# Weight tiles issued ahead of the loads of v, conversions ungated and below attention, two groups ahead of the loop

## The chip, the cores and the metric

The kernel runs on one core of a Trainium2 chip (trn2). The time is that of one execution on the device in microseconds (us); it is compared as a median over several executions. TensorE (PE in the profile) multiplies matrices, VectorE (DVE) and ScalarE (ACT) work on elements, GpSimd (POOL) makes the constants, and SyncE (SP) issues every DMA, in one queue and in program order. Each engine executes its own instructions strictly in the order in which they were put down.

## What is computed

A block-sparse attention over 2 batches, 8 heads, 768 positions and a head size of 64, then two feed-forward layers over the 1536 tokens of 512 features:

```python
    k_sum = k.reshape(B, H, nb, block, D).max(axis=3)      # nb = 24 blocks of 32
    v_sum = v.reshape(B, H, nb, block, D).mean(axis=3)
    scores_l = scale * np.matmul(q, k.transpose(0, 1, 3, 2))
    mask_l = np.abs(pos[:, None] - pos[None, :]) < window  # window = 16
    scores_s = scale * np.einsum('bhsd,bhnd->bhsn', q, k_sum) + np.log(block)
    a = softmax(np.concatenate([np.where(mask_l, scores_l, -1e9), scores_s], axis=-1))
    x = np.matmul(a, np.concatenate([v, v_sum], axis=2))
    ...
    h = np.maximum(x @ w_in, 0.0)                          # d_ff = 2048
    x = h * h @ w_out
    ...
    xn = x / rms * rms_g
    g = xn @ w_gate                                        # d_ff = 1536
    out = g * sigmoid(g) * (xn @ w_val) @ w_out2
```

The weights come as 64-bit floats and are converted on the chip.

## The kernel before

**Attention** goes by groups of 128 tokens, twelve in all (g = 0 to 11), six for each batch. For a batch, `prep_k` transposes k into `kT` (tiles `kps`) and takes its block maxima, and `vmean` averages v over blocks with matmuls (tile `vmean`, copied to `vm`). For each pair of groups `qprep` transposes q (`qps`). For each group `scores` multiplies (tiles `s`), `softmax` works on DVE and ACT (tile `t`), `ptrans` transposes the result (`pps`, copied to `pT`), and `av` multiplies it with the values (`xps`) and splits the sum into `xhi` (ACT) and `xlo` (DVE). The values of a group lie in `vx`, four slots that two groups share: `vload` brings the 96 rows of each half group from v, `vmfix` copies the 24 rows of summaries from `vm` into each slot. The rows of the summaries stay in the slots, so `vmfix` is called for the first two groups of a batch alone.

**The weights** pass through a list (`units1`): first `wi` 0 to 3 and `wo` 0 to 3, then the others. A tile is loaded raw in 512 KB (`load64`, lines 160 and 164). `tick()` then does one step for up to three tiles: `conv_a` (two instructions on ACT, lines 175 and 176), `conv_b` (four on DVE, lines 182, 183, 186 and 189) and `split` (a cast on ACT, line 195, and a subtraction on DVE, line 196). So one tile costs three instructions on ACT and five on DVE.

**The first layer** is worked in rounds over its 16 tiles of `d_ff`; the first round holds four. In it a step takes two groups at a time: `h` (48 matmuls of 256 columns for a pair of groups, `product`, line 621), `r` (relu on ACT, line 769, and the square on DVE, line 770), `hsplit` (`hhi` on ACT, line 632, `hlo` on DVE, line 633), and `y` (24 matmuls of 512 columns, `ff_out`, line 642). `h_0_0` is the first half of `h` for the pair of groups 0 and 1, `h_0_2` its second half, `y_0_0` and `y_0_1` are the sums of these two groups. While this round runs, `Attention.point` puts one step of the attention of later groups between the products. The other two rounds and the second layer (`g`, `v`, `z`) follow.

**What sets the order.** The program is written in one sequence, and a scheduler orders each engine's instructions by priority. Every call of `Attention.point` raises the priority of what it emits by `LIFT` instructions. `after(...)` holds the instructions of a block back until a marked instruction has been issued: before, ten ticks are gated in that way behind the exponentials, the transposes and the splits of groups 0 and 1. Three groups (0, 1 and 2) are written out by hand ahead of the loop, and the loop starts at group 3.

Memory for raw tiles and for converted tiles comes from one ring of 14 (`wpool`, tag "w"); a tile that is to be loaded waits until the tile that had its place has been read.

Of the kernel before, what the change touches and what calls it, by code (L numbers as in the profile page):

```python
# [32 lines left out]
def tile_window_attention_moe_moe2(  # L33
# [210 lines left out]
    def NENG(g):  # L244
# [3 lines left out]
    QB = 2  # L248
    E0, E1 = 2, 3
    GN = (3, 1, 2, 1)  # L250
    GATES = sum(
        (
            [g] * n
            for g, n in zip(
                (
                    (("exp", 1), ("norm", 1)),
                    (("pT", 1), ("norm", 1)),
                    (("xhi", 0, 1), ("xlo", 0, 1)),
                    (("xhi", 1, 1), ("xlo", 1, 1)),
                ),  # L260
                GN,
            )
        ),
        [],
    )
    WARM, VM1 = 10, 1
    LIFT, POINTS = 120, 5
    WOLAG = 2
# [25 lines left out]
    NVX = 4  # L294
    vx = [ap_.tile([NK, H, D], F32, name=f"vx{i}") for i in range(NVX)]
    psX = actx.enter_context(tc.tile_pool(name="psX", bufs=2, space=PSUM))
# [113 lines left out]

    def vmfix(g):
        if g % GPB >= NVX // 2:
            return
        vm = state["vm"].rearrange("n (h d) -> n h d", h=H)
        for u in range(2):
            t = vx[(2 * g + u) % NVX]
            for j, a in ((WIN, u), (K0 + QT, 1 - u)):
                nc.sync.dma_start(t[j : j + GAP], vm[GAP * a : GAP * (a + 1)])

    def vload(g):  # L420
        b, r = divmod(g, GPB)
        for u in range(2):
            t = vx[(2 * g + u) % NVX]
            t0 = r * P + u * QT
            for j, n, o in ((0, WIN, t0 - WIN), (K0, QT, t0), (K1, WIN, t0 + QT)):
                o = min(max(o, 0), S - n)
                nc.sync.dma_start(t[j : j + n], v[b, :, o : o + n, :].rearrange("h s d -> s h d"))  # L427

# [73 lines left out]
    def av(g):  # L502
        pT = state.pop(("pT", g))
        ps = psA(f"xps1_{g}")
        for u in range(2):
            for p in range(NPAIR):
                o = p * P + QT * u
                for e in range(2):
                    nc.tensor.matmul(  # L509
                        ps[QT * e : QT * e + QT, o : o + QT],  # L510
                        vx[(2 * g + u) % NVX][:, 2 * p + e, :],
                        pT[:, e * NPAIR + p, QT * u : QT * u + QT],
                        start=True, stop=True,
                    )
# [9 lines left out]
    def pieces(g):  # L524
# [37 lines left out]
        def sc():  # L562
            scores(g)
            vload(g)
            softmax(g)
            vmfix(g)

# [11 lines left out]
    class Attention:  # L579
# [3 lines left out]
        def point(self, limit):  # L583
# [7 lines left out]
            for s_ in self.live:  # L591
# [3 lines left out]
                if need is None:  # L595
                    if s_.g >= limit:
                        continue
                elif not all(k_[0] in ("scores", "av") and k_[1] < 3 or k_ in state for k_ in need):
                    continue
# [12 lines left out]

    att = Attention(3)

# [86 lines left out]
    for c in range(NC2):  # L701
        prep_load(0, c)
    qload(0)
    for c in range(NC2):
        if c < E0:
            units1.load(c + 1)
        vm_load(0, c)
    for j in (0, LK - WIN):
        nc.gpsimd.memset(kT[:, :, j : j + WIN], 0.0)
# [5 lines left out]
    qprep(0)  # L715
    for c in range(VM1):
        vmean(0, c)
    prep_kend(0, 1)
    scores(0)
    with after(("s", 0)):  # L720
        for c in range(VM1, NC2):
            vmean(0, c)
    vload(0)
    vmfix(0)
    vload(1)
    vmfix(1)
    qload(2)
    softmax(0)
    with after(("s", 0)):
        scores(1)  # L730
    units1.ahead = 0
    for _ in range(E1):
        units1.tick()
    qprep(2)
    ptrans(0)
    softmax(1)
    scores(2)
    av(0)
    ptrans(1)
    vload(2)  # L740
    av(1)
    rot["tags"] = ("a", "x")
    softmax(2)
    ptrans(2)
    av(2)
    units1.ahead = 6
    for t in GATES:
        with after(*t):
            units1.tick()

# [175 lines left out]
```

## Time and profile before

| | |
|---|---|
| time, median of 3 runs | 704.88 us (701.39 to 708.34) |
| the profiled execution | 704.73 us, its span 703.0 us |
| instructions | 9371 |
| mean granted clock of TensorE | 0.969 |
| PE, DVE, ACT busy in the span | 668.5 us (95%), 408.4 us (58%), 307.2 us (44%) |

The span reaches from the first to the last instruction; 1.73 us of the execution lie around it. PE is busy for 95% of the span, which is an average over a beginning that is not bound by PE and a long rest that is, so the stretches are read one by one.

### The profile page before, as it was taken

To read this page: it belongs to the slowest core of one execution; us is meant where nothing else is said; L and a number is where in the kernel's file an instruction comes from. 1 tells how busy PE (TensorE), PEld (TensorE's weight loads), DVE (VectorE), ACT (ScalarE), POOL (GpSimd) and SP (SyncE) were. 2 spreads that over 40 slices of the span, in tenths; PEclk is the share of its full clock that TensorE was granted. 3 is DMA by queue.
4 is the path that set the end of the run, shared out by engine and by line. 5 is a ranking of instruction groups with operands and counts; after the bars stand their busy time and mean duration, and the time that the engine had idled before them with its cause. 6 is when DMAs were issued, how large, how long until landed. Compare 5 with 4: busy or idle time off the path is not lost.

```text
span 703.0 us, 9371 instructions
## 1 busy us (share of the span) xinstructions
PE 668.5 (95%) x3644; PEld 540.3 (77%) x3644; DVE 408.4 (58%) x735; ACT 307.2 (44%) x624; POOL 4.0 (1%) x25
## 2 busy tenths in 40 slices
PE   6687899888999999999999999999999999999997
PEld 5375676677888888888888888888888888888885
DVE  4798655555699938952838398349932152213122
ACT  4663254665576625622635486246721132111110
POOL 2000000000000000000000000000000000000000
PEclk9958799999999999999999999999999999999999
DMA  9589135222370321300114025014300000001011
GB/s 246 122 256 249 24 88 179 57 74 68 102 229 0 121 90 60 91 30 1 61 54 126 19 76 176 0 51 131 119 1 0 1 1 0 1 0 61 1 60 61
DMA packets 78236, 54.22 MB, mean 77 GB/s; under 512 B 46128, under 2 KB 72752, under 8 KB 78192
## 3 DMA queue, kind: packets, MB, share of 16 engines
q1 hardware_dynamic: 78192, 53.62, 25.9%
q8 instruction: 29, 0.48, 0.3%
q14 instruction: 15, 0.12, 0.1%
HBM read 50.07 MB, written 3.15 MB: 76 GB/s over the span
## 4 chain that ended last, share of the span: by engine, by line
PE 84%; ACT 4%; DVE 4%; SPq 4%; DMA 3%; issue 1%; DVEq 0%; ACTq 0%
PE y L642 18%; PE h L621 16%; PE g L621 14%; PE v L621 14%; PE z L642 14%; ACT t L468 3%; PE xps L509 2%; SPq L427 2%; DMA raw_wi<-in_moe_w_in_dram 2%; PE s L439 2%; SPq L327 1%; PE pps L488 1%; DVE t L462 1%; PE vmean L401 1%; PE xps L521 1%
## 5 line engine op out<-in xcount | busy, mean ns | idle before, releaser
L621 PE MATMUL h<-xhi,w_wi 128*128 128x512 f32 (+1 forms) x480 | 135.3, 356 | 0.8 <-ACT xhi L499 0.7
L642 PE MATMUL y<-w_wo,hhi 128*128 128x512 f32 x384 | 122.5, 404 | 7.7 <-ACT hhi L632 4.7
L872 DVE TENSOR_TENSOR sg<-v,sg 128x512 f32<-128x512 f32 x36 | 24.9, 692 | 132.8 <-PE v L621 132.8
L621 PEld LDWEIGHTS h<-xhi,w_wi 128*128 128x128 f32 x480 | 86.8, 195 | 13.9 <-ACT xhi L499 1.2
L621 PE MATMUL g<-xhi,w_wg 128*128 128x512 f32 x288 | 95.7, 393 | 0.0
L621 PE MATMUL v<-xhi,w_wv 128*128 128x512 f32 x288 | 95.7, 393 | 0.0
L642 PEld LDWEIGHTS y<-w_wo,hhi 128*128 128x128 f32 x384 | 73.0, 192 | 25.6 <-ACT hhi L632 5.1
L642 PE MATMUL z<-w_wp,hhiz 128*128 128x512 f32 x288 | 88.6, 392 | 0.0
L621 PE MATMUL h<-xlo,w_wi 128*128 128x512 f32 (+1 forms) x240 | 85.6, 357 | 1.6 <-DVE xlo L500 1.6
L642 PE MATMUL y<-w_wo,hlo 128*128 128x512 f32 x192 | 75.8, 402 | 1.6 <-DVE hlo L633 1.6
L870 ACT ACTIVATE sg<-g 128x512 f32<-128x512 f32 x36 | 21.5, 598 | 100.6 <-PE g L621 100.3
L621 PEld LDWEIGHTS g<-xhi,w_wg 128*128 128x128 f32 x288 | 54.1, 188 | 12.4
L621 PEld LDWEIGHTS v<-xhi,w_wv 128*128 128x128 f32 x288 | 54.1, 188 | 12.2
L642 PEld LDWEIGHTS z<-w_wp,hhiz 128*128 128x128 f32 x288 | 54.1, 188 | 11.9
L769 ACT ACTIVATE r<-h 128x512 f32<-128x512 f32 x48 | 28.5, 595 | 65.9 <-PE h L621 65.9
L621 PE MATMUL g<-xlo,w_wg 128*128 128x512 f32 x144 | 56.7, 394 | 0.0
L621 PE MATMUL v<-xlo,w_wv 128*128 128x512 f32 x144 | 56.6, 393 | 0.0
L642 PE MATMUL z<-w_wp,hloz 128*128 128x512 f32 x144 | 55.4, 393 | 0.0
L621 PEld LDWEIGHTS h<-xlo,w_wi 128*128 128x128 f32 x240 | 46.7, 194 | 8.1 <-DVE xlo L500 1.9
L632 ACT CAST hhiz<-sg 128x512 fp32r<-128x512 f32 x36 | 22.3, 620 | 66.4 <-DVE sg L872 66.0
L770 DVE TENSOR_TENSOR r<-h,r 128x512 f32<-128x512 f32 x48 | 32.9, 688 | 28.0 <-ACT r L769 27.9
L642 PEld LDWEIGHTS y<-w_wo,hlo 128*128 128x128 f32 x192 | 36.5, 192 | 10.1 <-DVE hlo L633 2.0
(125 smaller groups left out, 916.3 us busy)
## 6 DMA issues: line engine op xcount, KB each, us to landing
raw_wi<-in_moe_w_in_dram SPq DMA_DIRECT2D x16, 512.0 KB
raw_wo<-in_moe_w_out_dram SPq DMA_DIRECT2D x16, 512.0 KB
raw_wg<-in_moe_w_gate_dram SPq DMA_DIRECT2D x12, 512.0 KB
raw_wv<-in_moe_w_val_dram SPq DMA_DIRECT2D x12, 512.0 KB
raw_wp<-in_moe_w_out_dram SPq DMA_DIRECT2D x12, 512.0 KB
kr<-in_k_dram SPq DMA_DIRECT2D x12, 256.0 KB
qr<-in_q_dram SPq DMA_DIRECT2D x12, 256.0 KB
vr<-in_v_dram SPq DMA_DIRECT2D x6, 512.0 KB
```

Source lines behind the costliest of these rows:

```text
L327: nc.sync.dma_start(t[:, j].rearrange("p (h d) -> p h d", h=H), src[b, :, o : o + P, :].rearrange("h p d -> p h d"),)
L427: nc.sync.dma_start(t[j : j + n], v[b, :, o : o + n, :].rearrange("h s d -> s h d"))
L439: mark[("s", g)] = nc.tensor.matmul(sl[e][QT * u : QT * u + QT, p, :], qT[rr, p, QT * u : QT * u + QT], kT[rr, p, o : o + NK], start=True, ...
L468: mark[("exp", g)] = nc.scalar.activation(t[:, h], t[:, h], AF.Exp, bias=mx[:, h : h + 1], accum_out=sm[:, h : h + 1])
L509: nc.tensor.matmul(ps[QT * e : QT * e + QT, o : o + QT], vx[(2 * g + u) % NVX][:, 2 * p + e, :], pT[:, e * NPAIR + p, QT * u : QT * u + QT ...
L621: nc.tensor.matmul(ps, a_, b_, start=(i == 0), stop=(i == tot - 1))
L632: nc.scalar.copy(hi[:, 0:n], s[:, 0:n])
L642: nc.tensor.matmul(y, a_[:, ms], b_, start=(first and i == 0), stop=(last and i == 2))
L769: nc.scalar.activation(t, ps, AF.Relu)
L770: nc.vector.tensor_tensor(t, ps, t, op=ALU.mult)
L870: nc.scalar.activation(t, psg, AF.Silu)
L872: nc.vector.tensor_tensor(t, psv, t, op=ALU.mult)
```

## The change

Six weight tiles instead of two are asked for before anything of attention runs: `wi` 0 and 1 now ahead of the loads of v for the means (they lay between them before), and `wi` 2 and 3, `wo` 0 and 1 right behind these (they were loaded as the gated ticks came). The four `vx` tiles become one tile with four slots, so that for the first batch `vmfix` writes the summaries of two groups with one transfer (4 instead of 8; for the second batch they stay 8). The gates on the ticks go; after group 1 eight pairs of one attention step and one tick follow (`HEAD`). Two groups, not three, are written out ahead of the loop. `LIFT` rises from 120 to 300.

```diff
-    E0, E1 = 2, 3
-    GN = (3, 1, 2, 1)
-    GATES = sum(
...
-    WARM, VM1 = 10, 1
-    LIFT, POINTS = 120, 5
+    E0, E1, HEAD = 2, 6, 8
+    WARM = 10
+    LIFT, POINTS = 300, 5
...
-    vx = [ap_.tile([NK, H, D], F32, name=f"vx{i}") for i in range(NVX)]
+    vx = ap_.tile([NK, NVX, H, D], F32, name="vx")
...
+    def vmfix(i0, n):
+
+        vt = vx.rearrange("k (i u) h d -> k u i (h d)", u=2)
         for u in range(2):
-            t = vx[(2 * g + u) % NVX]
             for j, a in ((WIN, u), (K0 + QT, 1 - u)):
-                nc.sync.dma_start(t[j : j + GAP], vm[GAP * a : GAP * (a + 1)])
+                rows = state["vm"][GAP * a : GAP * (a + 1)]
+                nc.sync.dma_start(
+                    vt[j : j + GAP, u, i0 : i0 + n], rows.unsqueeze(1).to_broadcast([GAP, n, DM])
+                )
...
-                elif not all(k_[0] in ("scores", "av") and k_[1] < 3 or k_ in state for k_ in need):
+                elif not all(k_ in state for k_ in need):
...
     qload(0)
+    units1.load(E0)
     for c in range(NC2):
-        if c < E0:
-            units1.load(c + 1)
         vm_load(0, c)
+    units1.load(E1)
...
     vload(0)
-    vmfix(0)
+    vmfix(0, NVX // 2)
     vload(1)
-    vmfix(1)
-    qload(2)
     softmax(0)
     with after(("s", 0)):
         scores(1)
     units1.ahead = 0
-    for _ in range(E1):
-        units1.tick()
-    qprep(2)
+    units1.tick()
+    softmax(1)
+    units1.tick()
     ptrans(0)
-    softmax(1)
-    scores(2)
     av(0)
     ptrans(1)
-    vload(2)
     av(1)
     rot["tags"] = ("a", "x")
-    softmax(2)
-    ptrans(2)
-    av(2)
-    units1.ahead = 6
-    for t in GATES:
-        with after(*t):
-            units1.tick()
+    for g in range(2):
+        state[("scores", g)] = state[("av", g)] = True
+    units1.ahead = E1 + 2
+    att = Attention(2)
+    for _ in range(HEAD):
+        att.point(NG)
+        units1.tick()
```

How the order of the instructions moves is seen at three places.

**SP's queue.** Before, the raw tiles `wi` 2 and 3 and `wo` 0 stand behind the loads of `vx` for group 2, the first of which waits for `av` of group 0:

```order
L427 DMA vx_86<-in_v_dram 16x8x64
L427 DMA vx_87<-in_v_dram 16x8x64
L427 DMA vx_87<-in_v_dram 64x8x64
L427 DMA vx_87<-in_v_dram 16x8x64
L160 DMA raw_wi_500<-in_moe_w_in_dram 128x4x256
L160 DMA raw_wi_502<-in_moe_w_in_dram 128x4x256
L164 DMA raw_wo_504<-in_moe_w_out_dram 128x1024
```

After, these tiles stand ahead of the loads of q for groups 2 and 3 and of all `vx`:

```order
L300 DMA vr_2_125<-in_v_dram 128x8x128
L160 DMA raw_wi_127<-in_moe_w_in_dram 128x4x256
L160 DMA raw_wi_129<-in_moe_w_in_dram 128x4x256
L164 DMA raw_wo_131<-in_moe_w_out_dram 128x1024
L164 DMA raw_wo_133<-in_moe_w_out_dram 128x1024
L311 DMA qr_400<-in_q_dram 128x8x64 x2
L412 DMA vx<-in_v_dram 16x8x64
```

and three more raw tiles stand between the loads of `vx` for groups 0 and 1 and the summaries:

```order
L412 DMA vx<-in_v_dram 64x8x64
L412 DMA vx<-in_v_dram 16x8x64
L164 DMA raw_wo_414<-in_moe_w_out_dram 128x1024
L164 DMA raw_wo_416<-in_moe_w_out_dram 128x1024
L160 DMA raw_wi_418<-in_moe_w_in_dram 128x4x256
L401 DMA vx<-vm_244 12x2x512 x4
L311 DMA qr_545<-in_q_dram 128x8x64 x2
```

So the four transfers of the summaries moved behind nine weight tiles in all.

**DVE, where the softmax of group 2 begins.** Before, its first addition (tile `t_446`, from `s_2`) follows that of group 1 directly:

```order
L462 TENSOR_TENSOR t_348<-s_1_285,mask_mid 128x480
L462 TENSOR_TENSOR t_348<-s_1_286,mask_mid 128x480
L466 TENSOR_REDUCE mx_349<-t_348 128x4 x2
L462 TENSOR_TENSOR t_446<-s_2_369,mask_mid 128x480
L462 TENSOR_TENSOR t_446<-s_2_370,mask_mid 128x480
```

After (tile `t_468`) it stands behind the conversion of six tiles and among that of the last three; `x_wo_555` and `x_wo_579` are `wo` 2 and 3, `x_wi_609` is `wi` 4:

```order
L186 SCALAR_TENSOR_TENSOR x_wo_555<-raw_wo_414,x_wo_555 128x512
L183 TENSOR_SCALAR x_wo_579<-x_wo_579 128x512
L182 TENSOR_SCALAR x_wi_609<-x_wi_609 128x512
L189 ISA x_wo_555<-x_wo_555,u_wo_556 128x1024
L186 SCALAR_TENSOR_TENSOR x_wo_579<-raw_wo_416,x_wo_579 128x512
L183 TENSOR_SCALAR x_wi_609<-x_wi_609 128x512
L449 TENSOR_TENSOR t_468<-s_2_444,mask_mid 128x480
L189 ISA x_wo_579<-x_wo_579,u_wo_580 128x1024
L196 TENSOR_TENSOR w_wo_602<-x_wo_555,w_wo_602 128x512
```

So the softmax of group 2 moved back past the conversions of `wi` 2, `wi` 3, `wo` 0 and `wo` 1, in among those of the next three tiles.

**PE, at the transposes of groups 4 and 5.** Before, they (`pps` of `t_742` and `t_778`) stand within `h_1_2`, and `av` of group 4 and the transposes of k for the second batch follow; `y_1` comes only 70 rows later, and a quarter of `y_0` too:

```order
L621 MATMUL h_1_2_1089<-xhi_0_404,w_wi_537 128x256 x2
L488 MATMUL pps_0_864<-ident,t_778 120x128 x4
L621 MATMUL h_1_2_1089<-xlo_0_405,w_wi_537 128x256
L621 MATMUL h_1_2_1089<-xhi_0_404,w_wi_537 128x256
L509 MATMUL xps_4_842<-pT_797,vx_86 64x64
L488 MATMUL pps_1_870<-ident,t_778 120x128 x3
L509 MATMUL xps_4_842<-pT_797,vx_86 64x64 x7
```

After, all of `y_1` precedes the transposes of group 4 (`t_721`):

```order
L629 MATMUL y_1_0_1530<-w_wo_602,hlo_1_2_1169 128x512
L629 MATMUL y_1_1_1531<-w_wo_602,hlo_1_2_1169 128x512
L629 MATMUL y_1_0_1530<-w_wo_626,hhi_1_2_1168 128x512 x2
L629 MATMUL y_1_0_1530<-w_wo_626,hlo_1_2_1169 128x512
L629 MATMUL y_1_1_1531<-w_wo_626,hhi_1_2_1168 128x512 x2
L629 MATMUL y_1_1_1531<-w_wo_626,hlo_1_2_1169 128x512
L475 MATMUL pps_0_809<-ident,t_721 120x128 x4
L475 MATMUL pps_1_815<-ident,t_721 120x128 x4
L475 MATMUL pps_0_843<-ident,t_757 120x128 x4
L496 MATMUL xps_4_821<-pT_808,vx 64x64
```

So the products of the first two pairs moved forward, ahead of the second half of the first batch's attention. From the scores of groups 8 and 9 (`s_8`, `s_9`) on, both programs have the same steps in nearly the same order on PE.

## Rows read from the trace of the kernel before

**Rows 1.** The page: granted clock of TensorE in tenths, 40 slices of 17.6 us

```profile
PEclk9958799999999999999999999999999999999999
```

**Rows 2.** Stretches (us): busy time and instructions of each engine, granted clock, DMA share, GB/s

```profile
10.00:20.00 10.00, 6.97 (x76) 3.13 (x74) 6.68 (x14) 6.15 (x14) 0.00 (x0) 1.00 1.03 299
14.58:49.60 35.02, 25.05 (x228) 16.48 (x228) 28.26 (x62) 21.86 (x61) 0.00 (x0) 0.75 0.76 214
49.60:86.55 36.95, 29.96 (x194) 24.18 (x194) 28.07 (x45) 13.53 (x22) 0.00 (x0) 0.73 0.55 135
86.55:140.95 54.40, 50.33 (x480) 38.38 (x478) 31.80 (x56) 30.27 (x76) 0.00 (x0) 1.00 0.39 105
140.95:184.30 43.35, 38.75 (x375) 32.20 (x376) 23.31 (x37) 25.88 (x90) 0.00 (x0) 0.96 0.22 58
184.30:700.00 515.70, 514.53 (x2281) 420.70 (x2279) 292.19 (x529) 208.83 (x366) 0.00 (x0) 1.00 0.18 57
```

**Rows 3.** PE's timeline: start, us, instruction, idle time before it and who ended it

```profile
26.93 0.66 PE L388 MATMUL qps<-ident,qr 128*128 128x128 f32 x4 [3.46 <-DMA qr<-in_q_dram]
...
49.61 0.58 PE L621 MATMUL h<-xhi,w_wi 128*128 128x256 f32 x1
...
61.24 1.20 PE L642 MATMUL y<-w_wo,hhi 128*128 128x512 f32 x4 [2.96 <-ACT hhi L632]
...
64.03 1.22 PE L642 MATMUL y<-w_wo,hlo 128*128 128x512 f32 x2 [1.59 <-DVE hlo L633]
```

**Rows 4.** SP's timeline: its DMA issues

```profile
14.69 9.14 SPq L427 DMA_DIRECT2D vx<-in_v_dram  x12
...
25.05 6.29 SPq L418 DMA_DIRECT2D vx<-vm  x8
31.91 3.55 SPq L427 DMA_DIRECT2D vx<-in_v_dram  x6
35.50 0.98 SPq L160 DMA_DIRECT2D raw_wi<-in_moe_w_in_dram  x2
```

**Rows 5.** DVE's timeline

```profile
14.58 0.43 DVE L182 TENSOR_SCALAR x_wi<-x_wi 128x512 f32<-128x512 f32 x1 [3.07 <-ACT x_wi L175]
...
17.85 0.65 DVE L462 TENSOR_TENSOR t<-s,mask_first 128x480 f32<-128x480 f32 x1
18.42 0.64 DVE L466 TENSOR_REDUCE mx<-t 128x4 f32<-128x480 f32 x1
...
30.87 1.22 DVE L462 TENSOR_TENSOR t<-s,mask_mid 128x480 f32<-128x480 f32 x2 [4.97 <-PE s L439]
...
59.49 0.42 DVE L183 TENSOR_SCALAR x_wi<-x_wi 128x512 uint32<-128x512 uint32 x1
59.82 0.69 DVE L186 SCALAR_TENSOR_TENSOR x_wo<-raw_wo,x_wo 128x512 uint32<-128x512 uint32 x1
60.42 1.15 DVE L475 TENSOR_REDUCE sm<-t 128x8 f32<-128x960 f32 x1
61.48 0.69 DVE L186 SCALAR_TENSOR_TENSOR x_wi<-raw_wi,x_wi 128x512 uint32<-128x512 uint32 x1
```

**Rows 6.** PE's timeline at the full clock: attention's steps

```profile
103.09 4.47 PE L401 MATMUL vmean<-vr,ind 128*24 128x512 f32 x10
...
112.75 1.91 PE L439 MATMUL s<-kT,qT 64*64 64x120 f32 x48
...
128.27 1.06 PE L488 MATMUL pps<-ident,t 128*120 128x128 f32 x8 [0.97 <-DVE t L478]
...
134.97 2.08 PE L509 MATMUL xps<-pT,vx 120*64 120x64 f32 x62
...
138.62 2.33 PE L439 MATMUL s<-kT,qT 64*64 64x120 f32 x64
```

**Rows 7.** The chain that ended last, in order of time: products at the full clock

```profile
101.48 1.67 PE h L621 x14
...
281.92 2.80 PE y L642 x12
```

More of the change, by code (lines that the diff above doesn't have):

```diff
@@ L248, in tile_window_attention_moe_moe2 @@
     QB = 2
-    E0, E1 = 2, 3
-    GN = (3, 1, 2, 1)
-    GATES = sum(
[L252 to L265, printed above, removed]
-    WARM, VM1 = 10, 1
-    LIFT, POINTS = 120, 5
+    E0, E1, HEAD = 2, 6, 8
+    WARM = 10
+    LIFT, POINTS = 300, 5
     WOLAG = 2
@@ L409, in vmean @@
             state[("vsum", b)] = True
[L411 to L414, printed above, removed]
+    def vmfix(i0, n):
+        vt = vx.rearrange("k (i u) h d -> k u i (h d)", u=2)
         for u in range(2):
-            t = vx[(2 * g + u) % NVX]
             for j, a in ((WIN, u), (K0 + QT, 1 - u)):
-                nc.sync.dma_start(t[j : j + GAP], vm[GAP * a : GAP * (a + 1)])
+                rows = state["vm"][GAP * a : GAP * (a + 1)]
+                nc.sync.dma_start(
+                    vt[j : j + GAP, u, i0 : i0 + n], rows.unsqueeze(1).to_broadcast([GAP, n, DM])
+                )
     def vload(g):
         b, r = divmod(g, GPB)
+        i0 = 2 * g % NVX
         for u in range(2):
-            t = vx[(2 * g + u) % NVX]
             t0 = r * P + u * QT
@@ L426, in vload @@
                 o = min(max(o, 0), S - n)
-                nc.sync.dma_start(t[j : j + n], v[b, :, o : o + n, :].rearrange("h s d -> s h d"))
+                nc.sync.dma_start(
+                    vx[j : j + n, i0 + u], v[b, :, o : o + n, :].rearrange("h s d -> s h d")
+                )
     def scores(g):
@@ L510, in av @@
                         ps[QT * e : QT * e + QT, o : o + QT],
-                        vx[(2 * g + u) % NVX][:, 2 * p + e, :],
+                        vx[:, (2 * g + u) % NVX, 2 * p + e, :],
                         pT[:, e * NPAIR + p, QT * u : QT * u + QT],
@@ L565, in sc @@
             softmax(g)
-            vmfix(g)
+            if r < NVX // 2:
+                vmfix(g % (NVX // 2), 1)
         yield sc, 1, [("av", g - 2), ("qT", g), ("vsum", b), ("scores", g - 1)]
@@ L611, in until @@
                 self.point(NG)
-    att = Attention(3)
     def mm3(ps, pairs):
@@ L715, in tile_window_attention_moe_moe2 @@
     qprep(0)
-    for c in range(VM1):
-        vmean(0, c)
     prep_kend(0, 1)
@@ L720, in tile_window_attention_moe_moe2 @@
     with after(("s", 0)):
-        for c in range(VM1, NC2):
+        for c in range(NC2):
             vmean(0, c)
     vload(0)
-    vmfix(0)
+    vmfix(0, NVX // 2)
     vload(1)
-    vmfix(1)
-    qload(2)
     softmax(0)
```

## The prediction

> **What bounds the kernel now.** I read the stretches first, since the 95% of the page is an average. From 184.3 to 700 us PE works 514.5 of 515.7 us at full clock [rows 2]: nothing that the change does in the beginning can shorten that part, it can only let it start earlier. What is left is in front. From 14.58 to 49.6 PE does attention for three groups and waits 10.0 of 35.0 us; the first product stands at 49.61 [rows 2, 3]. From 49.6 to 86.55 it waits 7.0 of 37.0 us and has a mean granted clock of 0.73; from 86.55 to 140.95 it waits 4.1 us at full clock [rows 2]. The slices show where the clock falls to its lower level of 1.2 GHz: around 35 to 53 us and again for parts of 53 to 88 us [rows 1].
>
> Then I asked which wait ends last there. DVE is the busiest beside PE: 28.3 of 35.0 us before the first product [rows 2], and 5.0 of the missing 6.8 us are one wait, for the scores of group 2 [rows 5], which waited for q (3.46 us on PE, row at 26.93) [rows 3]. In the next stretch PE waits 2.96 us for `hhi` and 1.59 us for `hlo` [rows 3], which ACT and DVE deliver late because the conversions of `wo` stand between. These tiles were asked for late: their loads are issued from 35.50 on, behind the loads of `vx` at 31.91 that wait for `av` of group 0 [rows 4]. So until 86 us the bound is DVE's list of work together with late weights, and PE's clock suffers from the waits.
>
> **The prices.** On DVE what counts is the step from one start to the next: 0.33 us for the two short steps of a conversion (59.49 to 59.82), 0.60 for the long ones (59.82 to 60.42), 1.06 for a step of the softmax over eight heads (60.42 to 61.48) and 0.57 over four (17.85 to 18.42) [rows 5]. A converted tile is thus 2 x 0.33 + 3 x 0.60 = 2.5 us of DVE. On PE at full clock a matmul of `h` is 1.67 / 14 = 0.119 us, one of `y` 2.80 / 12 = 0.233 [rows 7], a transpose 1.06 / 8 = 0.13, a pair of `scores` 2.33, `av` of one group 1.04, `vmean` 0.447 a record [rows 6].
>
> **The loads.** Before, 5.9 MB (k, q, two weight tiles, v for the means, `vx`, q again) were in when `qps` began at 26.93 [rows 3]. Now 2.1 MB of weights go ahead of the last two of these; at 299 GB/s [rows 2] that is 7 us, so q for group 2 and `vx` are in by some 34 us. The three further tiles that stand ahead of the summaries are 1.6 MB, 5.3 us: the summaries land at about 39.5, where the loads behind `av` of group 0 were issued from 31.91 before [rows 4]. This looks like a new wait of 8 us, but DVE decides: it comes to the first addition of group 2's softmax only at 42.5 (next part). Late summaries cost nothing up to about 41, and each us beyond costs one. That the summaries come in 4 transfers saves 4 of the 8 issues of 0.79 us [rows 4] on a queue that is not late; I cost it at nothing, and at most at 3.1 us either way, since each transfer now writes twice the rows. Moving `wi` 1 ahead of v for the means delays the latter by 1.8 us at the same rate; `vmean` is not needed before the summaries, so nothing.
>
> **The head, on DVE.** It starts on `wi` 0 at 14.58 [rows 5], which stands at the same place in SP's queue. From the order, up to the last step of the first half of group 2's softmax it has eight tiles (8 x 2.5 = 19.8), four steps of `wi` 4 (1.9), two softmaxes in halves (4 x 1.9 = 7.6, a half being three steps of 0.57 and two small ones), that half of group 2 (five steps, 3.1) and two `xlo` (1.2): 33.6 us, to 48.2; I add 1.8 us for waits on ACT's exponentials and casts, an allowance. At 50.0 PE transposes the half (0.5), and at about 50.7 the products of the first pair run freely. Before that was 49.61. So the head gains nothing, it even loses 1.1 us, and `av` of group 2 is still to do; but all eight tiles are converted, where before the conversions of `wo` ran on beside the first products (59.49 to 61.48) [rows 5].
>
> **From there to the scores of groups 8 and 9,** which end at 138.62 + 2.33 = 140.95 before [rows 6], and behind which both programs have the same steps. PE's work in between, at full clock: 142 `h` (16.9), 72 `y` (16.8), `av` of six groups (6.3), 44 transposes of `t` (5.8), 48 of k and q (6.4), three pairs of `scores` (7.0), `vmean` (5.4): 64.6 us. The same prices give 48.6 us for what PE did from 86.55 to 140.95, where 50.3 were busy [rows 2], so I take 3.5% more: 67.0. Waits: DVE delivers `hhi` for `y_0` about 1.1 us late behind the softmaxes of groups 2 and 3 (it lies in PE's slow start, 0), `hhi` and `hlo` for `y_1` twice 1.1, and one large: between the end of `s_7` and the transposes of group 6, DVE has 8.4 us of steps (softmax 6 and 7 with three conversions between) and some 1.5 of exponentials, while PE has only 19 `h` and 12 `y` left (5.1), as `y_0` and `y_1` are spent. That is 5 us, and 0.5 behind it: 7.7 in all. Before, 13.6 us lay from 114.66 to 128.27 there [rows 6], filled by these products.
>
> **The clock.** From 49.6 to 86.55 PE was busy for 29.96 us [rows 2] with what my prices make 17.1: half rate and fine interleaving cost 12.9. Now PE comes out of the waiting head at the lower level too, which costs at least 2 us until the products have brought it back; at most as much as before, 12.9. I take 5: the waits at 61.24 and 64.03, ahead of one of the two falls [rows 1, 3], go; sparse attention steps remain.
>
> Sum: 67.0 + 7.7 + 5 = 79.7 from 50.7, so 130.4 in place of 140.95: 10.5 us earlier. The span becomes 692.5, and with the 1.7 us around it 694. The profiled execution (704.73) stands at the median (704.88), so no correction.
>
> The bounds: with 2 us for the clock, no 3.5% and half the waits it is 9 us less, 685; with 12.9 for the clock 702. Conversions below attention in priority move some tiles (`wi` 5 to 8) a little later; from the order their casts stand behind the last `xlo` of attention as before, so nothing.
>
> **Rivals.** *The clock gives it all back* (0.14). PE idles in the head while DVE converts nine tiles and waits again before group 6; if the lower level costs the 12.9 us that it cost before, 702, no change. For it: the lower level held for the whole third slice [rows 1]. Against it: 86.55 to 140.95 ran at full clock in spite of 4.1 us of waits [rows 2]. The Trainium skill, "TensorE: Matmul & The Clock Gate" (HAM oscillation), says that a matmul stretch shorter than the wait ahead of it runs at half rate each time anew; by that rule the price is the upper one, 702, and the trace agrees with it for the stretch before 86 us alone.
>
> *The softmax of groups 6 and 7 binds* (0.12). If the stretch from the end of `s_7` to the start of `s_8` takes its 24 us of before (114.66 to 138.62) [rows 6] and not my 17.5, because raw tiles of the second round hold ACT and DVE there, 6.5 us are lost: 700.5, within 1%.
>
> *Slower: half clock through the first two pairs* (0.06). If the level stays at 1.2 GHz from 50.7 until `y_1` is done, 31 us of priced work take twice as long: 26 us in place of the 5, 720. It makes the kernel slower by 1% once more than some 23 us are added, three quarters of that stretch. Against it: dense products brought the level back within the slice each time [rows 1].
>
> That the change does not do what it says is partly so: the order shows conversions in front of group 2's softmax although they are lower in priority, since ACT and DVE had them ready first; the sum has that in it.
>
> **How the numbers follow.** The forecast's case, 694, has 0.68. The range from 685 to 703 takes in the first two rivals and leaves out the third and the far ends, under 0.2. A measurement of this kernel tells about 1% from no change. Faster by over 1% (below 697.8) is the forecast's case, 0.68; within 1% are the first two rivals, 0.26; slower 0.06.
>
> **What would show it.** In the profile after: the first `xps` at 37 to 41 us, ended by a DMA; the dense products from about 51; DVE without a long wait from 14.6 to 50; `y_0` complete by 70 and `y_1` ahead of the transposes of group 4 at 85 to 90; one wait of about 5 us for `t` before the transposes of group 6; the scores of groups 8 and 9 done near 130; and behind it the same stretch as before. It is wrong if the summaries land after 41 us, if the granted clock is low between 55 and 90 us, or if the part behind the scores of groups 8 and 9 changes length.

## The result and the profile after

Before 703.97 us (median of 20 runs, 701.39 to 709.53), after 707.41 us (20 runs, 706.19 to 711.94); the ratio is 1.0055 with a 95% interval of 1.0036 to 1.0074. The change makes the kernel 0.55% slower, where 694.0 was forecast. The profiled execution of the changed kernel took 706.91 us with a span of 705.1. The two profiled executions thus lie 2.2 us apart and the medians 3.4, so the pieces below account for the smaller of the two.

The stretches of the changed kernel: head up to the free products (those that follow each other without a wait, from 53.81 on), products of the first two pairs, up to the end of the scores of groups 8 and 9, rest of attention, dense part. The cuts are at the same places of the program as in [rows 2], but for the one at 92.20: the cut at 86.55 there lies within the products of the second pair.

```profile
14.58:53.40 38.82, 22.22 (x180) 13.42 (x180) 34.73 (x74) 25.74 (x67) 0.00 (x0) 0.65 0.77 215
53.40:92.20 38.80, 34.00 (x294) 28.20 (x295) 27.86 (x43) 12.94 (x21) 0.00 (x0) 1.00 0.37 91
92.20:139.56 47.36, 41.52 (x414) 31.28 (x412) 24.31 (x46) 27.87 (x70) 0.00 (x0) 0.93 0.52 134
139.56:186.27 46.71, 40.40 (x378) 33.28 (x377) 24.99 (x40) 27.66 (x93) 0.00 (x0) 0.93 0.19 50
186.27:702.10 515.83, 514.44 (x2281) 420.31 (x2279) 291.48 (x526) 207.22 (x363) 0.00 (x0) 1.00 0.18 58
```

The dense part has its length of before (515.83 beside 515.70 in [rows 2]). In front of it the changed kernel is 2.0 us late (186.27 beside 184.30), in three pieces: the free products begin 4.2 us later than before, the scores of 8 and 9 nevertheless end 1.4 us earlier (139.56 beside 140.95), and the rest of attention is 3.4 us longer (46.71 beside 43.35).

PE's timeline after, at the places of [rows 3, 6]:

```profile
37.22 0.44 PE L475 MATMUL pps<-ident,t 128*120 128x128 f32 x1 [9.13 <-DVE sm L464]
...
41.56 1.73 PE L496 MATMUL xps<-pT,vx 120*64 120x64 f32 x26 [2.40 <-DMA vx<-vm]
43.22 1.86 PE L426 MATMUL s<-kT,qT 64*64 64x120 f32 x16
...
53.81 0.36 PE L608 MATMUL h<-xlo,w_wi 128*128 128x256 f32 x1
...
85.64 1.20 PE L629 MATMUL y<-w_wo,hhi 128*128 128x512 f32 x4 [1.66 <-ACT hhi L619]
...
92.21 1.47 PE L475 MATMUL pps<-ident,t 128*120 128x128 f32 x12
...
111.37 2.37 PE L426 MATMUL s<-kT,qT 64*64 64x120 f32 x64
...
124.34 1.93 PE L475 MATMUL pps<-ident,t 128*120 128x128 f32 x8 [5.62 <-DVE t L465]
125.92 2.05 PE L629 MATMUL y<-w_wo,hhi 128*128 128x512 f32 x4
...
136.98 2.59 PE L426 MATMUL s<-kT,qT 64*64 64x120 f32 x64
```

In the head PE stands 9.13 us before the first half of group 1's transposes, then 2.40 us for the summaries; the scores of group 2 come behind both, at 43.22, and reach DVE at 45.13, which had them at 30.87 before [rows 5]. The product `y_1` starts at 85.64, in time with the forecast, and is long done when PE waits 5.62 us for the softmax of group 6. The four `y` matmuls behind that wait take 2.05 us and not 1.20: the clock is at its lower level.

SP's issues after, beside [rows 4]:

```profile
22.92 9.82 SPq L412 DMA_DIRECT2D vx<-in_v_dram  x12
32.86 0.83 SPq L164 DMA_DIRECT2D raw_wo<-in_moe_w_out_dram  x2
33.78 0.38 SPq L160 DMA_DIRECT2D raw_wi<-in_moe_w_in_dram  x1
34.26 3.49 SPq L401 DMA_DIRECT2D vx<-vm  x4
```

The 12 loads of `vx` hold the queue until 32.74, and the summaries, in 3.49 us and not 6.29, come only behind three more tiles.

DVE at the scores of groups 8 and 9, after and then before. After, the four additions of both groups stand in front of both maxima; before, one group was finished first:

```profile
138.90 2.35 DVE L449 TENSOR_TENSOR t<-s,mask_mid 128x480 f32<-128x480 f32 x4 [0.49 <-PE s L426]
141.17 2.20 DVE L453 TENSOR_REDUCE mx<-t 128x8 f32<-128x960 f32 x2
```

```profile
139.70 1.22 DVE L462 TENSOR_TENSOR t<-s,mask_mid 128x480 f32<-128x480 f32 x2 [0.81 <-PE s L439]
140.96 1.15 DVE L466 TENSOR_REDUCE mx<-t 128x8 f32<-128x960 f32 x1
142.03 1.21 DVE L462 TENSOR_TENSOR t<-s,mask_mid 128x480 f32<-128x480 f32 x2
```

The first maximum began 0.01 us behind the end of the scores before (140.95), and 1.61 us behind it after (139.56).

### The profile page after: what moved, and what is told of

Read it like the earlier page. It is cut to its first block, busy times and chain, and to the rows that moved or that the text cites. A ratio compares the mean times of both kernels' runs of the same rounds, so it can differ in the third digit from the quotient of the medians.

```text
span 705.1 us, 9364 instructions
## 1 busy us (share of the span) xinstructions
PE 663.8 (94%) x3644; PEld 536.5 (76%) x3644; DVE 408.0 (58%) x735; ACT 308.2 (44%) x624; POOL 4.0 (1%) x25
## 4 chain that ended last, share of the span: by engine, by line
PE 85%; DVE 5%; ACT 4%; DMA 2%; SPq 2%; issue 1%; DVEq 0%
PE y L629 19%; PE h L608 16%; PE g L608 14%; PE v L608 14%; PE z L629 14%; PE xps L496 3%; ACT t L455 2%; PE pps L475 1%; PE s L426 1%; DVE t L449 1%; DMA raw_wi<-in_moe_w_in_dram 1%; DMA vx<-vm 1%; SPq L311 1%; PE qps L372 1%; PE vmean L385 1%; SPq L300 1%
## 5 line engine op out<-in xcount | busy, mean ns | idle before, releaser
L608 PE MATMUL h<-xhi,w_wi 128*128 128x512 f32 (+1 forms) x480 | 132.5, 351 | 0.0
L608 PEld LDWEIGHTS h<-xhi,w_wi 128*128 128x128 f32 x480 | 84.6, 190 | 13.7 <-issue 1.3
```

The costliest lines, as they stand in the source:

```text
L608: nc.tensor.matmul(ps, a_, b_, start=(i == 0), stop=(i == tot - 1))
```

## The experiments

Theory A: PE alternates between the scores of two groups, and both softmaxes end late. Theory B: late summaries shift everything. When both fell, theory C: attention is a chain of its own, and products only fill it, against D: PE's own work sets the pace. Each experiment is given by its ratio to the kernel before, with the 95% interval.

**Pairs apart.** In `pieces`:

```diff
+            with after(("s", g - 1)):
-            scores(g)
+                scores(g)
```

> The changed kernel with one addition: the scores of a group may not be issued before the last score of the group in front of it, so that two groups no longer stand row by row between each other on PE (score pairs 4/5, 6/7, 8/9 and 10/11) and DVE adds and reduces one group before it begins the next. Theory A (the time is lost because the new start lets two groups' attention steps become ready together, so that PE alternates between their scores and DVE finishes both before either softmax can start): the stretch from the end of the scores of groups 8/9 to the dense run of h_5 goes back from 46.7 us to 43.3 to 44, the middle (first products to the end of those scores, 85.8 us) loses 2 to 4 us of its alternations; 5 to 7 us in all, median 700 to 703, ratio to before 0.995 to 0.999. Rival B (the time is lost ahead of the first products: the summaries of v land at 41.9 behind three raw weight tiles, and everything behind is shifted): the first products stand at 53.8 as in the changed kernel and the median stays at 706 to 708, ratio 1.004 to 1.007.

Measured: 1.0060 (1.0030 to 1.0089), 708.82 us: no gain, by the ratio in B's range and not in A's. The edit does what it is for behind group 7 (table below), but the scores of 6 and 7 end at 119.54 and not 113.74, since `y_1` now stands in front of the k transposes.

**Summaries first.** The loads of `wo` 2, `wo` 3 and `wi` 4 are gated behind the last transfer of `vmfix`.

```diff
+        if i == 0:
+            with after("vmfix"):
+                units1.load(E1 + 3)
```

> The changed kernel with one move in SP's queue: the four transfers of the summaries stand ahead of the loads of wo 2, wo 3 and wi 4, not behind them; six tiles are still early. Rival B: the summaries land by 38 to 39 instead of 41.9, the first product moves from 53.8 to 50 to 51, and the end moves with it: 704, ratio 1.000 to 1.002. Theory A: the first product moves by the same 3 us, but the pairs of scores stay interleaved (the alternations on PE are as many), so the tail of attention keeps its 46.7 us and the middle gives part of the gain back in waits for converted tiles, which come later: 705 to 708, ratio 1.002 to 1.006.

Measured: 1.0118 (1.0075 to 1.0162), 713.18 us, slower than the changed kernel and than either theory had it. The summaries are issued from 32.81, the first product of all is at 46.95 and not 50.08 (the free products, of which the expectation speaks, at 48.51 and not 53.81), and the end is later. B falls.

**Both edits.**

> Both edits: scores of a group behind those of the group in front, and the summaries ahead of the three tiles. If A and B are both right and add up: 3 us in front, 3 us in the tail, 2 to 4 us in the middle, 697 to 700, ratio 0.990 to 0.995. If only A: as the run with the pairs apart alone. If only B: as the run with the summaries first alone.

Measured: 1.0028 (1.0002 to 1.0053), 708.31 us: not a sum, and not between the two either. By the ratio it is below each edit alone; its interval overlaps those of the pairs apart and of the changed kernel.

**Three groups ahead** of the loop, as before the change; all else of the change stays.

```diff
+    qload(2)
+    qprep(2)
     ptrans(0)
+    scores(2)
+    vload(2)
     av(0)
 ...
+    softmax(2)
+    ptrans(2)
+    av(2)
-    att = Attention(2)
+    att = Attention(3)
```

> The changed kernel with three groups written ahead of the loop again (as before the change), everything else of the change kept: six tiles early, summaries in 4 transfers behind the three tiles, conversions ungated. It asks what the choice of two groups is worth. Theory A: score pair 4/5 is no longer interleaved, pairs 8/9 and 10/11 still are; the middle loses 2 to 3 us, the tail stays at 46 to 47: 704 to 706, ratio 0.999 to 1.003. Rival B: the summaries land as late or later (one more load of q stands ahead of them), the first product at 54 or later: 706 to 709, ratio 1.004 to 1.008.

Measured: 0.9961 (0.9931 to 0.9992), 702.49 us: faster than both kernels, by 0.9% than the changed one. That is more than either theory expected.

**`y_1` held**: its products behind the scores of group 7 (`with after(("s", 7))` around `ff_out` where `k_ == 1`).

> The changed kernel with one reordering on PE: the 24 matmuls of y_1 (the second products of groups 2 and 3) may not be issued before the last score of group 7; they lay ahead of the transposes of group 4. No work is left out. Theory C (attention is a chain of its own, scores, softmax, transposes, average, next scores, of some 25 us a pair of groups; products only fill it, so products that run early are missing later as filler): PE waits some 3 us more before the transposes of group 4, the chain comes earlier, the scores of groups 6 and 7 end 3 to 5 us before 113.7, the wait of 5.6 us before the transposes of group 6 is filled by y_1, and the end moves by 2 to 5 us: median 702.5 to 705.5, ratio 0.998 to 1.002. Rival D (PE's own work and alternations set the pace, what was on PE early is gained): the wait that goes at 118.7 comes back where y_1 lay, no change: 706 to 708.5, ratio 1.003 to 1.007.

Measured: 1.0047 (1.0022 to 1.0072), 707.91 us: no change, as D has it. DVE of this kernel from the end of the scores of 4 and 5 (77.83) on:

```profile
77.81 0.66 DVE L449 TENSOR_TENSOR t<-s,mask_mid 128x480 f32<-128x480 f32 x1 [1.81 <-PE s L426]
78.39 0.65 DVE L449 TENSOR_TENSOR t<-s,mask_last 128x480 f32<-128x480 f32 x1
78.95 0.65 DVE L449 TENSOR_TENSOR t<-s,mask_mid 128x480 f32<-128x480 f32 x1
79.52 0.65 DVE L449 TENSOR_TENSOR t<-s,mask_last 128x480 f32<-128x480 f32 x1
80.08 2.20 DVE L459 TENSOR_REDUCE mx<-t 128x8 f32<-128x960 f32 x2
...
89.06 1.16 DVE L465 TENSOR_TENSOR t<-t,sm 128x960 f32<-128x960 f32 x1
90.13 0.20 DVE L464 RECIPROCAL sm<-sm 128x8 f32<-128x8 f32 x1
90.36 1.16 DVE L465 TENSOR_TENSOR t<-t,sm 128x960 f32<-128x960 f32 x1
```

and what PE does meanwhile:

```profile
90.36 2.79 PE L475 MATMUL pps<-ident,t 128*120 128x128 f32 x12 [6.60 <-DVE sm L464]
```

With 5.5 us of products taken out of its way, the transposes of group 4 start 1.85 us earlier in the profiled execution (90.36 beside 92.21); the rest is the wait of 6.60. DVE runs both softmaxes through each other without a pause. C's mechanism is visible, its forecast of a gain fell: the hole moved.

**Two groups in the kernel before**: the edit of "three groups" backwards, in the kernel before, nothing else of the change.

> The kernel before with one part of the change: two groups instead of three are written ahead of the loop; late loads, gates, eight summary transfers stay. Theory C: with one group less done when the products begin, the chain of the pairs begins later and its products are spent earlier: 3 to 6 us slower than before, ratio 1.004 to 1.009. Rival D: the same work in another order, dense products start earlier: 0 to 4 us faster, ratio 0.994 to 1.000.

Measured: 1.0112 (1.0073 to 1.0151), 713.06 us: the way C has it, and by more.

```profile
34.64 0.58 PE L621 MATMUL h<-xhi,w_wi 128*128 128x256 f32 x1 [0.68 <-ACT xhi L499]
...
68.99 1.96 PE L488 MATMUL pps<-ident,t 128*120 128x128 f32 x8 [5.98 <-DVE t L478]
...
91.63 2.78 PE L488 MATMUL pps<-ident,t 128*120 128x128 f32 x12 [5.56 <-DVE t L478]
```

The first product comes 15 us earlier than in [rows 3] (34.64 beside 49.61) and the kernel is 1.1% slower: PE later waits 5.98 and 5.56 us for softmaxes. Between 41 and 56 us it also waits 5.8 us for converted weights, which the changed kernel does not.

**Products left out.**

```diff
-    W[("wo", f + j)], f + j == 0, f + j == ROUNDS1[0] - 1,
+    W[("wo", f + j)], f + j == 0, f + j == ROUNDS1[0] - 1, 1 if 1 <= k_ <= 3 else 3,
```

> The changed kernel with work left out: of the 24 matmuls of each of y_1, y_2 and y_3 only the 8 of the leading terms (high part by high part) are issued, 16 x 0.2315 = 3.7 us of PE less for each of three pairs, 11.1 us in all ahead of h_5. Theory C: the waits grow instead; the scores of groups 10 and 11 end 3 to 5 us before 165.6, and the median is 702 to 705, ratio 0.997 to 1.001. Rival D: PE's time goes down by what was left out: scores of 10 and 11 end 9 to 11 us earlier, median 696 to 699, ratio 0.988 to 0.992.

Measured: 0.9990 (0.9964 to 1.0016), 704.61 us. Of 11.1 us left out 2.8 (by the medians) to 4.6 us (by the ratios, 0.65% of 704) come back; the scores of 10 and 11 end at 161.13, 4.5 us earlier. The page counts the missing 48 matmuls, and the wait before the transposes of group 6 has grown from 5.62 to 6.73:

```profile
PE 657.1 (93%) x3596; PEld 531.5 (76%) x3596; DVE 408.3 (58%) x735; ACT 307.7 (44%) x624; POOL 4.0 (1%) x25
```

```profile
125.69 1.93 PE L475 MATMUL pps<-ident,t 128*120 128x128 f32 x8 [6.73 <-DVE t L465]
```

**Softmax shortened.**

```diff
+            if g >= 2:
+                continue
             nc.vector.tensor_scalar_add(s_, s_, 1e-9)
```

> The changed kernel with work of DVE left out and PE's left whole: from group 2 on the softmax stops behind the exponentials (no sum, no reciprocal, no division by the sum), so that a group is 2.6 us (groups 2 to 5) or 1.6 us (groups 6 to 11) shorter on DVE. Theory C (the chain of scores, softmax, transposes, average and next scores sets the pace, PE is in it only with its attention steps): 5 us less for each of the pairs 2/3 and 4/5, 2 to 3 for each later pair, of which some comes back as waits elsewhere: 9 to 15 us faster than the changed kernel, median 692 to 698, ratio 0.983 to 0.991. Rival D (PE's work and alternations set the pace): 0 to 4 us, 703 to 707.5.

Measured: 0.9911 (0.9883 to 0.9938), 697.61 us, 1.4% faster than the changed kernel, as C has it. The page of this kernel, and of the changed one:

```profile
PE 667.1 (96%) x3644; PEld 537.0 (77%) x3644; DVE 390.1 (56%) x697; ACT 306.0 (44%) x624; POOL 4.0 (1%) x25
```

```profile
PE 663.8 (94%) x3644; PEld 536.5 (76%) x3644; DVE 408.0 (58%) x735; ACT 308.2 (44%) x624; POOL 4.0 (1%) x25
```

DVE has 17.9 us less (390.1 beside 408.0), PE the same 3644 matmuls, and some 10 us come back. A us of the softmax on DVE is worth more than half a us here, a us of PE's products 0.25 to 0.4. What was left out on DVE lies between the exponentials and the transposes, so the run shows what the chain is worth, not what any work of DVE is. The Trainium skill ("Perfetto Trace Analysis", Identifying the Most-Contended Engine) says to optimize the engine with the highest occupancy first, and judges TensorE by MFU (the share of its peak arithmetic) or by the busy share of its weight loads. By the latter the engine here is TensorE, with weight loads (PEld) at 76% beside DVE at 58%; the two runs show the softmax on DVE to be the better place as long as attention lasts.

**Three groups, pairs apart.**

> The changed kernel with three groups written ahead of the loop (as in the run of that name) and with the scores of a group behind those of the group in front. Theory A for the tail alone: pairs 6/7, 8/9 and 10/11 were still interleaved there; the softmax of the first of a pair begins 1.5 us earlier each time: 2 to 4 us faster than with three groups alone, 698 to 701, ratio 0.990 to 0.995. Rival: as with two groups, what the tail gains the middle gives back: 701 to 703.5, ratio 0.995 to 0.998.

Measured: 0.9932 (0.9904 to 0.9961), 700.43 us, in A's range for the tail; the interval overlaps that of three groups alone.

**Two groups, pairs apart, `y_1` held.**

> The changed kernel with both reorderings: scores of a group behind those of the group in front, and y_1 behind the scores of group 7. With the pairs apart alone the transposes of group 4 came 9.6 us behind the scores of 4/5 and not 14.2, but y_1 then lay between the transposes of 4 and 5 and the k transposes of the second half began at 102 and not at 95.5; with y_1 held alone the interleaved softmax of 4/5 (12.5 us) filled the hole. Theory C: each edit takes away what ate the other's gain, the k transposes begin at 94 to 96, the scores of 8/9 end at 136 to 139 and the wait of 6 us before the transposes of group 6 is filled: 4 to 6 us faster than either alone, median 702 to 705, ratio 0.997 to 1.001. Rival D: as each alone, 706 to 709, ratio 1.003 to 1.006.

Measured: 1.0043 (1.0020 to 1.0066), 706.69 us: as each alone, though the profiled execution shows the scores of 6 and 7 at 114.09 and not 119.54. C missed again on a rearrangement of products.

**Three groups, pairs apart, `y_1` held.**

> The changed kernel with three groups written ahead of the loop, the pairs apart and y_1 held behind the scores of group 7. Theory C: the wait of 5.3 us before the transposes of group 6 goes and the k transposes come earlier by as much as y_1 stood in front of them: 2 to 5 us faster than three groups with the pairs apart (700.4): 695.5 to 698.5, ratio 0.986 to 0.991. Rival D: the same as that, 700 to 701, ratio 0.993 to 0.995.

Measured: 0.9920 (0.9897 to 0.9943), 697.75 us. The best version, 0.8% faster than before; not told apart from the one without the hold.

**The same with the summaries first.**

> As three groups, apart and held, and with the summaries ahead of wo 2, wo 3 and wi 4 in SP's queue. Theory B, which fell for two groups ahead (the first products came 5 us earlier and the end 6 us later), would give 2 to 3 us more here: 693 to 696. Theory C: the averages of groups 0 and 1 are no link of the chain, since the scores of 2 and 3 already stand ahead of them, so nothing, or a loss where the order behind them changes: 695 to 700.

Measured: 1.0068 (1.0045 to 1.0091), 708.68 us, 1.5% slower than without that edit. In the order the scores of group 3 now stand behind `h_0` and among `y_0`; the scores of 4 and 5 end at 89.31 and not 75.64.

**Of the third group only q and the scores and softmax ahead** (two groups otherwise, pairs apart).

> The changed kernel with the pairs apart and, of the third group, only q's transposes, the scores, the loads of v and the softmax written ahead of the loop, in front of the average of group 0; its transposes and average are left to the stream, as in the changed kernel. If the link that costs is that the scores of group 2 stand behind the waits for group 1's softmax and the summaries: as three groups with the pairs apart, 699.5 to 703, ratio 0.992 to 0.997. If it is that the average of group 2 must lie ahead of the products: as two groups with the pairs apart, 706 to 709, ratio 1.003 to 1.008.

Measured: 1.0047 (1.0018 to 1.0076), 709.15 us, as two groups with the pairs apart. That the scores of group 2 come late is not, by itself, what costs.

**Three groups, pairs apart, three early tiles** (`E1 = 3`).

> Three groups ahead with the pairs apart (700.4), less one part of the change: three weight tiles and not six are loaded ahead of v, the others come behind the loads of v. If the early tiles carry a gain as the forecast had it (products no longer wait for late weights): 3 to 8 us slower than with them, 703.5 to 708.5, ratio 0.998 to 1.006. Theory C: the products only fill, their weights have time: within 1.5 us, 699 to 702, ratio 0.991 to 0.996.

Measured: 1.0022 (0.9995 to 1.0048), 706.17 us: 0.9% slower than with six early tiles. C's number falls: in this order the early tiles do carry a gain. But it is not that PE waits for late weights: between 30 and 200 us it waits 0.2 us in all for converted tiles. The loss is at one place, the softmax of group 6. With three early tiles:

```profile
115.27 0.45 SPq L164 DMA_DIRECT2D raw_wo<-in_moe_w_out_dram  x1
118.83 0.66 ACT L175 ACTIVATE x_wo<-raw_wo 128x512 f32<-128x512 f32 x1 [3.13 <-DMA raw_wo<-in_moe_w_out_dram]
119.39 0.38 ACT L455 ACTIVATE t<-t,mx 128x120 f32<-128x120 f32 x1
126.55 1.93 PE L475 MATMUL pps<-ident,t 128*120 128x128 f32 x8 [8.94 <-ACT t L455]
```

and with six (three groups, pairs apart):

```profile
115.55 0.45 SPq L164 DMA_DIRECT2D raw_wo<-in_moe_w_out_dram  x1
115.10 0.40 ACT L455 ACTIVATE t<-t,mx 128x120 f32<-128x120 f32 x1 [1.14 <-DVE mx L453]
122.68 1.93 PE L475 MATMUL pps<-ident,t 128*120 128x128 f32 x8 [5.34 <-DVE t L465]
```

The raw `wo` is asked for at the same time in both. With three early tiles ACT has its conversion in front of the exponentials of group 6 and waits 3.13 us for it; with six it stands behind them. PE's wait ahead of the transposes is 3.6 us longer, of 3.8 us that lie between the two profiled executions (705.79 and 701.97). Such a wait of ACT is not a loss in every order: the best version (three groups, pairs apart, `y_1` held) has one of 4.14 us at 115.1.

**The kernel before with six early tiles** (`units1.load(6)` behind the loads of v for the means).

> The kernel before with one part of the change: six weight tiles are loaded ahead of the loads of v for the attention windows, gates, three groups ahead and eight summary transfers as they were. The forecast's reason (late weights make PE wait 3 us for hhi and 1.6 for hlo at 58 to 64 us and keep its clock low): 4 to 8 us faster than before, ratio 0.988 to 0.995. Theory C: those waits go, the end moves by less than 2 us either way, ratio 0.997 to 1.003.

Measured: 1.0040 (1.0011 to 1.0069), 708.07 us: slower, against the forecast's reason; the interval reaches into C's range. The scores of 4 and 5 end 1.3 us earlier than before, those of 6 and 7 3.7 us later (table).

The places in the profiled executions, in us. "Second stage" is the first transpose behind the norm; behind it all are alike. Each row is one execution, up to 3.3 us away from the median of its kernel.

| kernel | first product | scores 4/5 end | scores 6/7 end | second stage | from scores 6/7 | ratio |
|---|---|---|---|---|---|---|
| before | 49.61 | 80.19 | 114.67 | 346.66 | 232.0 | 1 |
| after | 50.08 | 78.04 | 113.74 | 348.66 | 234.9 | 1.0055 |
| pairs apart | 49.28 | 81.17 | 119.54 | 351.86 | 232.3 | 1.0060 |
| summaries first | 46.95 | 79.13 | 117.49 | 354.73 | 237.2 | 1.0118 |
| both edits | 48.77 | 78.43 | 117.78 | 350.33 | 232.6 | 1.0028 |
| three groups | 46.99 | 75.39 | 108.77 | 344.68 | 235.9 | 0.9961 |
| `y_1` held | 49.84 | 77.83 | 114.95 | 348.68 | 233.7 | 1.0047 |
| before, two groups | 34.64 | 80.12 | 115.05 | 351.63 | 236.6 | 1.0112 |
| three, apart | 47.91 | 79.74 | 112.84 | 343.81 | 231.0 | 0.9932 |
| two, apart, held | 50.10 | 79.76 | 114.09 | 346.38 | 232.3 | 1.0043 |
| three, apart, held | 46.93 | 75.64 | 108.60 | 342.51 | 233.9 | 0.9920 |
| the same, summaries first | 44.35 | 89.31 | 118.71 | 352.30 | 233.6 | 1.0068 |
| scores of 2 ahead, apart | 45.58 | 80.70 | 118.42 | 350.47 | 232.1 | 1.0047 |
| three, apart, three tiles | 49.82 | 76.11 | 113.48 | 347.03 | 233.6 | 1.0022 |
| before, six tiles | 42.08 | 78.87 | 118.32 | 350.68 | 232.4 | 1.0040 |

The first product says nothing of the end: the four kernels with the earliest one (34.64, 42.08, 44.35, 45.58) are slower than before. From the end of the scores of 6 and 7 to the second stage the eight kernels with the pairs apart took 231.0 to 233.9 us, five with interleaved pairs (after, summaries first, three groups, `y_1` held, before with two groups) 233.7 to 237.2, 3.0 us more in the mean. The kernel before with six tiles, interleaved at 8/9 alone, took 232.4. In four pairs of kernels the edit that sets the pairs apart is the only difference (after, summaries first, three groups and `y_1` held, each without and with it): this stretch is 1.4 to 4.9 us shorter with the edit each time, yet the ratio moves by -0.9% to +0.05%, since what lies in front of it moves too.

## Why the prediction was wrong

Of the signs that the forecast named, `y_1` at 85.64, the wait of 5.62 us before group 6 and the full clock from 53.40 on came. The summaries (41.56 and not by 41), the scores of 8 and 9 (139.56 and not near 130) and the length behind them (46.71 beside 43.35) went against it.

**Head: 50.7 forecast, 53.8 measured, +3.1.** The list on DVE was nearly right in its steps (34.7 us busy up to 53.35, 33.6 forecast), but the allowance of 1.8 us for waits was 4.1: one wait of 1.46 us at 45.13 is for the scores of group 2. They stood behind the average of group 0, which waited for the summaries; these let it start at 41.56, not 39.5, since the loads of `vx` took until 32.74 to issue. The landing was 2 us off, and the rule "nothing up to about 41, each us beyond costs one" gives 0.6 us for it where the wait was 1.46. Yet two of the three runs that put the summaries first are slower for it, and the third is not told apart: even a head mended in this way is not a gain.

**Middle: 79.7 us forecast, 85.75 measured (53.81 to 139.56), +6.1.** Nearly all of it is in one stretch, from the end of the scores of group 7 to the start of those of group 8: 23.2 us (113.74 to 136.98), where I had 17.5 and [rows 6] have 24. That is the time of my second rival, which had 0.12, but not by its reason, raw tiles that hold up ACT and DVE in the softmax of group 6. That half came as forecast: 10.6 us to the transposes of group 6, 5.62 of them a wait, where I had 10.1 and 5. From there to the scores of group 8 it took 12.6 us and not 7.4. The window behind the wait, PE busy throughout at half the clock, 2.9 us lost:

```profile
124.34:130.18 5.84, 5.84 (x18) 4.97 (x19) 3.04 (x7) 2.57 (x5) 0.00 (x0) 0.50 0.36 108
```

and behind it PE alternates between two tiles row by row:

```profile
134.58 0.33 PE L496 MATMUL xps<-pT,vx 120*64 120x64 f32 x2
134.84 0.33 PE L372 MATMUL qps<-ident,qr 128*128 128x128 f32 x1
135.09 0.33 PE L496 MATMUL xps<-pT,vx 120*64 120x64 f32 x2
135.35 0.33 PE L372 MATMUL qps<-ident,qr 128*128 128x128 f32 x1
```

One such pair of rows takes 0.51 us (134.58 to 135.09); by the dense rows of [rows 6] two `xps` and a transpose are 2 x 2.08 / 62 + 1.06 / 8 = 0.20. By kinds the middle reads: waits 10.6 us (4.80 and 5.84 from the windows) and not 7.7; the clock 2.9 (the window above) and not 5, since it stayed up from 53.40 to 92.20; work at full clock the remaining 72.2 and not 67.0.

More than half of these 5.2 us of work is a slip in the forecast's own sum. Its allowance of 3.5% rests on 48.6 us for what PE did from 86.55 to 140.95. The trace of before has 84 `h`, 54 `y`, 72 transposes, `av` of four groups, two pairs of scores and 12 `vmean` there: by the forecast's prices 46.3 us, where 50.3 were busy. The allowance should have been 8 to 9%, which makes 70 us of the 64.6.

The rival that gives all back to the clock did not come: from 53.40 to 92.20 the granted clock was 1.00 in spite of waits up to 1.66 us. The same number rules out the reason of the third rival, half clock through the first two pairs; a slower kernel had 0.06 for that reason alone. The kernel that the Trainium skill describes ("TensorE: Matmul & The Clock Gate", HAM oscillation) has matmul stretches shorter than the waits between them, and each starts at the lower rate. That is not the case here: the four `y` matmuls at 85.64 take 1.20 us behind a wait of 1.66 us and run at the full clock, and behind the wait of 5.62 us, where the lower level came, PE worked on to 145.5.

**Behind the scores of 8 and 9: "the same steps", so the same length, was forecast; 46.71 beside 43.35, +3.4.** The steps are the same but not their order: both softmaxes run through each other, and the first maximum starts 1.6 us later behind the scores. 1.7 us of it are waits (6.31 beside 4.60) and 1.6 clock (0.93 of 46.71 us beside 0.96 of 43.35). With the pairs apart half of this piece or more comes back: from the end of the scores of 8 and 9 to the second stage the changed kernel took 209.1 us, before 205.7, the eight kernels with the edit 205.9 to 207.5. With three groups the sum gains too.

**The step that failed** is the sum from 50.7 on, which adds PE's work and a few waits and takes the part behind the scores of 8 and 9 as unchanged. Its terms against the trace: head +3.1, work at full clock +5.2, waits +2.9, clock -2.1, rest of attention +3.4, together 12.5 of the 12.6 us between the forecast span (692.5) and the measured one (705.1). Beside the sizes, the sum takes each us that PE gains for a us of the end. The two runs that leave work out show what it is worth there: a quarter to two fifths for PE's products, over half for DVE's softmax. The forecast's mechanism, late weights that make PE wait, shows no gain in the two runs that vary the early tiles alone: six of them are worth 0.9% in the three-group version, but through the order on ACT, and nothing or less in the kernel before.

**Which part made it slower** is shown from both sides: two groups ahead of the loop cost 0.9% in the changed kernel and 1.1% in the kernel before, where the waits for converted weights are part of the price. Without it the rest of the change gains 0.4%, and with the pairs apart 0.7%. I had costed the two groups only through DVE's list in front of group 2.

**What stays open.** Why two groups cost: it isn't the late scores of group 2 alone (the run that advances them gains nothing), and not the place of `y_1` alone. The stretch from the scores of 4/5 to those of 6/7, with the preparation of the second half in it, varies most, from 29.4 to 39.4 us over all kernels, without a rule that I could show. The four summary transfers, the missing gates and the higher `LIFT` were not tried by themselves.

## What to carry to other kernels

Where a chain through several engines lasts longer than the busiest engine's work in the same stretch, price an edit by what it does to the chain, and find out first, by leaving out work of each engine, whose us count. An earlier first product is no gain when it only spends the work that fills later waits. A part of a change that only writes code in another order moves every step behind it under a scheduler: compare the order behind the edit on every engine, down to which group's steps alternate, before "the same steps" is called the same time. And where a price list is calibrated on a measured stretch, count the rows of that stretch: here the miscount was worth 3 us.

## What the runs showed of the hardware

The scatter of one kernel's runs goes along with its mean granted clock: over the 20 runs of the changed kernel the time goes from 706.31 us at a mean clock of 0.973 to 711.94 at 0.962 (correlation -0.93, 0.45 us per 0.001), and of ten other kernels with 10 or more runs all but one show 0.3 to 0.5 us per 0.001. In both profiled executions (before and after) the lower level lies ahead of 178 us, but for the last few us. Whether the clock makes a run longer or longer waits lower the clock is not shown. A profile is one draw from that, so a difference of 2 us between two profiles is not by itself an effect; the pieces of the account above are those of one pair of executions.
